# Row sums inverted before the turn, spread by TensorE, and attention outputs transposed as bf16, in a fused attention and expert kernel

## The chip, the cores and the metric

The kernel runs on one core of one Trainium2 chip. The metric is device time in microseconds (us). Most executions of a kernel agree within 0.3%. "PE" is TensorE, "PEld" its weight loads, "DVE" VectorE, "ACT" ScalarE, "POOL" GpSimd, "SP" SyncE. The granted clock is the share of full speed at which TensorE was let run.

The kernels ran on more than one chip. The experiments e1 to e4 and e9 to e12 shared one chip, on which the kernel before takes 262.21 us in the first group and 261.33 us in the second. The experiments e5 to e8 ran on a slower chip, where it takes 270.59 us. So I compare ratios to the kernel before on the same chip, and lengths of stages inside one trace.

## The reference

Four batches of eight heads, 768 positions, head size 64. Each query sees the first 8 keys and the last 96, with a bias linear in the distance. The result, 3072 rows of 512, goes to eight experts. Each takes at most 384 rows, assigned greedily by gate logit.

```python
scores = scale * np.matmul(q, k.transpose(0, 1, 3, 2)) + bias      # bias = -slope[h] * distance
scores = np.where(keep, scores, -1000000000.0)                     # global or local keys only
a = np.exp(scores - np.max(scores, axis=-1, keepdims=True))
a = a / (np.sum(a, axis=-1, keepdims=True) + 1e-09)
x = np.matmul(a, v)                                                # then (tokens, heads * dim)
logits = x @ w_gate                                                # order = np.argsort(-logits.flatten())
out[mask_e] = np.maximum(x[mask_e] @ w1[e], 0.0) @ w2[e]           # for each expert e, at most 384 rows
```

## The kernel before

Attention works on sixteen pairs of heads, two pairs to a round `u`. A round makes scores in three groups; ScalarE takes the exponential; VectorE multiplies it by a mask with the bias in it; TensorE multiplies by `v` into `po` and, from the same masked values, makes the row sums and the gate products in one PSUM tile `pr`. ScalarE copies `po` to `oT` (features on partitions, not yet divided by the row sums). The row sums come back to one row per token by a VectorE transpose, so their reciprocal is small:

```python
def sums_out(n, pr):                      # per pair, VectorE
    LT = sp.tile([128, NBLK, 32], FP32, tag="LT")
    nc.vector.transpose(out=LT.rearrange("p b c -> p (b c)"), in_=pr)
    ri[n] = sp.tile([128, NBLK, 2], FP32, tag="ri", name=f"ri{n}", bufs=6)
    nc.vector.reciprocal(ri[n], LT[:, :, 16:18])            # 12 elements a partition
    nc.vector.tensor_tensor(out=Gb[b][...], in0=LT[:, :, 0:16]..., in1=ri[n]..., op=ALU.mult)
    # ... sums over pairs cut
def tok(n, hf):                           # six fp32 transposes a pair, in two halves
    pk = tokpool[0].tile([128, 3, 128], FP32, tag="pt", name=f"pk{n}_{hf}")
    for bb in range(3):
        nc.tensor.transpose(pk[:, bb, :], oTs[n][:, 3 * hf + bb]..., ident)
    return pk
def tok_out(n, hf, pk):                   # divide by the row sums while leaving PSUM, to bf16
    nc.vector.tensor_tensor(out=xs[u][...], in0=pk..., in1=ri[n]..., op=ALU.mult)
    # ... four writes of x to x_tok after the second pair of a round
```

The loop, rounds 2 to 6, in the order given to the engines:

```python
ps = scores(u, 0); expo(u, 0, ps)
kT(u + 1, 0); kT(u + 1, 1)                # transposes of the next k, VectorE
mask(2 * u, 0); mask(2 * u + 1, 0)
av(A); oT_out(A, 0); oT_out(A, 1)         # A, Bp: the two pairs of round u - 1
pr = sums(A)
# ... kA_out, qT, qT_out cut: copies of k and q by ScalarE
sums_out(A, pr)
ps = scores(u, 1); expo(u, 1, ps)
# ... cut
mask(2 * u, 1); mask(2 * u + 1, 1)
for hf in range(2): pk = tok(A, hf); tok_out(A, hf, pk)
av(Bp); oT_out(Bp, 0); oT_out(Bp, 1)
ps = scores(u, 2); expo(u, 2, ps); mask(2 * u, 2)
pr = sums(Bp); sums_out(Bp, pr)
mask(2 * u + 1, 2)
for hf in range(2): pk = tok(Bp, hf); tok_out(Bp, hf, pk)
```

After the loop a last round mixes attention with a first routing of five experts; then come further routing rounds and the experts. The PSUM pool `ps_t` has two buffers, both under the tag `pt`: `pr` and `pk` take turns in them. The scores have two tiles, `ps0` and `ps1`, of two banks each.

The softmax here doesn't subtract the row's maximum and nothing guards it: scores larger than these inputs give would overflow.

## Time and profile before

| | kernel before |
|---|---|
| time, median of 3 | 261.24 us (261.14 to 262.46) |
| span of the profiled execution, granted clock | 259.5 us, 0.989 |
| loop rounds, from first scores to first scores | 16.2 to 16.6 us, at clock 1.00 |
| first k transpose of round 2 | 38.49 us |
| last round, from its first scores to the first routing round | 116.45 to 145.80, so 29.35 us |
| first routing round | 145.80 to 152.06, so 6.26 us |
| from there to the end | 107.44 us |

The lines for this are in the prediction. They show a loop in which TensorE never stops, with VectorE and ScalarE close behind.

### The profile page before, as it was taken

Reading aid. Unit: us, or ns where it says so; the run is one execution under the profiler, and the core shown is the slowest. Engines: PE = TensorE matmul, PEld = TensorE weight load, DVE = VectorE, ACT = ScalarE, POOL = GpSimd, SP = SyncE. Lnnn points to the kernel's source line nnn. Section 1 sums busy time; section 2 is a strip of 40 time slices with the busy share of each in tenths; the row PEclk is TensorE's granted clock in tenths of the full one; section 3 lists DMA queues with packets and bytes.
Section 4 is the critical chain, followed back from the end, with each engine's and each line's share of the span. In section 5 each row is a group of like instructions: output and inputs, shape, how many; then the busy total and the mean of one; then the engine's idle time right before and its main releaser. Section 6 shows DMA issues by size and latency. Waiting matters only on the chain.

```text
span 259.5 us, 7844 instructions
## 1 busy us (share of the span) xinstructions
PE 241.5 (93%) x3331; PEld 180.0 (69%) x3331; DVE 163.0 (63%) x347; ACT 144.0 (55%) x245; POOL 88.3 (34%) x147
## 2 busy tenths in 40 slices
PE   8699979999999999999998999999999999999960
PEld 2467867888788888887787877765677775555520
DVE  3987998898878988679782687773232323223120
ACT  5998959779597795973432332323444442341600
POOL 5050000030180493005018301127884656742240
PEclk9999999999999999999999999999999999999995
DMA  7993597749689499958998999943599999994221
GB/s 259 328 329 79 160 254 207 197 87 279 185 219 269 81 236 244 198 121 131 208 210 180 168 194 204 201 126 98 96 185 252 262 241 275 231 208 180 83 85 47
DMA packets 52569, 49.29 MB, mean 190 GB/s; under 512 B 29744, under 2 KB 44080, under 8 KB 52528
## 3 DMA queue, kind: packets, MB, share of 16 engines
q0 software_dynamic: 15680, 26.22, 49.2%
q1 hardware_dynamic: 36848, 22.50, 31.7%
q8 instruction: 28, 0.46, 0.7%
q14 instruction: 13, 0.11, 0.1%
HBM read 56.05 MB, written 9.44 MB: 252 GB/s over the span
## 4 chain that ended last, share of the span: by engine, by line
PE 43%; DVE 20%; DMA 13%; issue 9%; ACT 8%; POOL 3%; SPq 1%; POOLq 0%; DVEq 0%
PE ph L1395 7%; PE po L443 6%; PE ps L390 6%; PE po L1404 5%; DVE RT L330 5%; DVE P L423 5%; DMA x_tok<-x 4%; DMA out_dram<-ot,idi 4%; POOL out_dram L955 3%; PE poE L998 3%; PE pr L474 3%; PE pk L519 3%; PE phE L982 2%; DMA RT<-x_tok,idiE 2%; DMA RT<-in_q_dram 2%
## 5 line engine op out<-in xcount | busy, mean ns | idle before, releaser
L408 ACT ACTIVATE P<-ps 128x860 f32<-128x860 f32 (+1 forms) x46 | 39.3, 893 | 23.1 <-PE ps L390 22.3
L1398 ACT ACTIVATE hT<-ph 128x256 bf16<-128x256 f32 (+1 forms) x64 | 27.1, 424 | 38.2 <-PE ph L1395 36.3
L390 PE MATMUL ps<-qT,kA 32*128 32x215 f32 (+2 forms) x864 | 43.2, 333 | 2.5 <-ACT qT L355 2.5
L390 PEld LDWEIGHTS ps<-qT,kA 32*128 32x128 f32 x864 | 36.8, 185 | 7.1 <-ACT qT L355 3.0
L443 PE MATMUL po<-P,v 128*64 128x215 f32 (+6 forms) x576 | 41.3, 293 | 0.1
L443 PEld LDWEIGHTS po<-P,v 128*64 128x64 f32 x576 | 34.1, 136 | 8.4 <-issue 3.2
L423 DVE TENSOR_TENSOR P<-P,Wm 128x860 f32<-128x860 f32 (+1 forms) x32 | 32.9, 1043 | 6.7 <-ACT P L408 4.0
L330 DVE STREAM_TRANSPOSE RT<-RT 128x768 f32<-128x768 f32 x28 | 26.2, 959 | 3.4 <-DMA RT<-in_k_dram 3.4
L474 PE MATMUL pr<-P,onesx 128*32 128x192 f32 (+11 forms) x768 | 27.6, 259 | 0.0
L1411 DVE COPY ot<-po 128x512 f32<-128x512 f32 x18 | 12.5, 692 | 23.9 <-PE po L1404 23.9
L955 POOL DMA_INDIRECT out_dram<-ot,idi x19 | 18.6, 981 | 23.2 <-DVE ot L1411 15.8
L474 PEld LDWEIGHTS pr<-P,onesx 128*32 128x32 f32 x768 | 24.7, 109 | 2.4 <-issue 0.3
L1404 PEld LDWEIGHTS <-hT 128*128 128x128 bf16 x152 | 14.4, 98 | 15.5
L340 ACT COPY kA<-RT 128x720 f32<-128x720 f32 (+2 forms) x18 | 24.4, 1354 | 0.2
L1404 PE MATMUL po<-w,hT 128*128 128x512 bf16 x104 | 23.8, 379 | 0.0
L1395 PE MATMUL ph<-xT,w 128*128 128x384 bf16 (+1 forms) x160 | 23.4, 305 | 0.0
L1376 DVE COPY xT<-pxe 128x512 bf16<-128x512 bf16 x17 | 6.6, 421 | 26.0 <-PE pxe L1375 25.6
L947 POOL DMA_INDIRECT xe<-x_tok,idi x19 | 18.3, 962 | 9.8 <-issue 3.7
L448 ACT COPY oT<-po 128x384 f32<-128x384 f32 x32 | 14.8, 491 | 11.2 <-PE po L443 11.2
L1395 PEld LDWEIGHTS <-w 128*128 128x128 bf16 x160 | 15.7, 98 | 7.7
L416 DVE TENSOR_TENSOR P<-P,Wm 128x860 f32<-128x860 f32 x16 | 16.4, 1058 | 6.6 <-ACT P L408 6.6
L519 PE MATMUL pk<-ident,oT 128*128 128x128 f32 x96 | 16.7, 287 | 2.4 <-DVE LT L490 2.2
(247 smaller groups left out, 330.4 us busy)
## 6 DMA issues: line engine op xcount, KB each, us to landing
w<-in_moe_w_dram POOLq DMA_DIRECT2D x10, 1024.0 KB, 11.9
v<-in_v_dram SPq DMA_DIRECT2D x32, 180.0 KB, 3.4
RT<-in_k_dram SPq DMA_DIRECT2D x7, 768.0 KB, 4.5
RT<-in_q_dram SPq DMA_DIRECT2D x7, 768.0 KB, 6.8
w_early<-in_moe_w_dram POOLq DMA_DIRECT2D x8, 512.0 KB, 7.9
x_tok<-x SPq DMA_DIRECT2D x32, 96.0 KB, 3.2
RT<-in_moe_w_dram POOLq DMA_DIRECT2D x2, 1024.0 KB, 18.4
w_early<-in_k_dram SPq DMA_DIRECT2D x1, 768.0 KB
```

What stands on the lines that cost most here:

```text
L330: nc.vector.transpose(out=t, in_=src[:, :, 32 * g : 32 * g + 32])
L340: nc.scalar.copy(out=kA[:, i0:i1, 8:128].rearrange("p i (c j) -> p i c j", j=NJ), in_=t[:, i0 * NC5 : i1 * NC5, :].rearrange("p (i c) j -> ...
L390: nc.tensor.matmul(heads[a][:, o : o + w], lhsT=kA[r, gd, i, :], rhs=qTt[r, gd, KT * i : KT * i + w], start=(gd == 0), stop=(gd == 1), ski ...
L408: nc.scalar.activation(P[:, :, 0 : GW[g]], ps[w_][:, :, 0 : GW[g]], AF.Exp, scale=0.125)
L423: tt(out=P[:, :, 0 : GW[g]], in0=P[:, :, 0 : GW[g]], in1=Wm[:, h0 : h0 + 2, lo : lo + GW[g]], op=ALU.mult)
L443: nc.tensor.matmul(po[n][bk][64 * t : 64 * t + 64, a - QB * bk : z - QB * bk], lhsT=v7[:, t, i, :], rhs=P[:, t, o + a - q0 : o + z - q0], ...
L474: nc.tensor.matmul(o_, lhsT=l_, rhs=r_, start=first[gq], stop=True, skip_group_check=True)
L519: nc.tensor.transpose(pk[:, bb, :], oTs[n][:, 3 * hf + bb].rearrange("c g r -> c (g r)"), ident)
L955: s = nc.gpsimd.indirect_dma_start(out=out[:, :], out_offset=bass.IndirectOffsetOnAxis(ap=ids, axis=0), in_=ot, in_offset=None)
L1395: nc.tensor.matmul(ph[:, 0 : 128 * ns], lhsT=w1_of(e)[:, kc, 128 * fc : 128 * fc + 128], rhs=xT_e[:, kc, 0:ns, :].rearrange("p t n -> p (t ...
L1398: nc.scalar.activation(hT[:, fc, 0 : 128 * ns], ph[:, 0 : 128 * ns], AF.Relu)
L1404: nc.tensor.matmul(po, lhsT=hT[:, fc, 128 * j : 128 * j + 128], rhs=w2_of(e)[:, fc, :], start=(fc == 0), stop=(fc == NFC - 1))
```

## The change

The intent is to take the twelve fp32 transposes of a round off TensorE. The row sums are inverted where they stand, on 192 columns (`rr`). A matmul with a selection matrix spreads them over the features' partitions, in the score banks, which are free for a moment (`R`). VectorE scales `oT` by this while casting it to bf16 (`xb`). TensorE transposes the bf16 tile six times into one bank (`pk`), and ScalarE copies that out as `x`. Pairs 12 to 15 keep the old way, for which their reciprocals are turned back (`rows_out`).

```diff
 def sums_out(n, pr):
-    nc.vector.transpose(out=LT.rearrange("p b c -> p (b c)"), in_=pr)
-    nc.vector.reciprocal(ri[n], LT[:, :, 16:18])
-    nc.vector.tensor_tensor(out=Gb[b][:, :, 2 * j : 2 * j + 2, :], in0=LT[...], in1=ri[n][...], op=ALU.mult)
+    nc.vector.reciprocal(rr[n], pr[:, 0, :])                                  # 192 elements a partition
+    nc.vector.tensor_tensor(out=gn, in0=pr[:, 1, :], in1=rr[n], op=ALU.mult)
+    nc.vector.transpose(out=Gb[b][:, j].rearrange("p b c -> p (b c)"), in_=gn)
+def rows_out(n):                     # pairs 12 to 15 only
+    nc.vector.transpose(out=LTr.rearrange("p b c -> p (b c)"), in_=rr[n])
+    nc.vector.tensor_copy(out=ri[n], in_=LTr...[:, :, :, 0])
+def spread(n):                       # pairs n and n + 1, into the score banks
+    R = [ps_s.tile([128, 2, 512], FP32, tag=f"ps{w_}", name=f"R{w_}_{n}") for w_ in range(2)]
+    for m in (n, n + 1):
+        for gq in range(4):
+            nc.tensor.matmul(R[gq // 2][:, gq % 2, o : o + 192], lhsT=selx[32 * gq : 32 * gq + 32, :],
+                             rhs=rr[m][32 * gq : 32 * gq + 32, :], start=True, stop=True, skip_group_check=True)
+def scale(n):
+    for w_ in range(2):
+        nc.vector.tensor_tensor(out=xbs[n][...], in0=oTs[n][...], in1=Rs[n][w_]..., op=ALU.mult)
+def turn_x(n): ...                   # six bf16 transposes of xbs[n] into one bank
+def x_out(n, pk):
+    nc.scalar.copy(out=xs[u][:, :, 128 * w_ : 128 * w_ + 128], in_=pk)
 # in round u:
 mask(2 * u, 0); mask(2 * u + 1, 0); av(A)
+spread(A - 2); scale(A - 2); scale(A - 1)
 # oT_out(A), pr = sums(A)
+pk = turn_x(A - 2)                   # x_out(A - 2, pk) among ScalarE's copies
 # sums_out(A, pr), second score group, second masks
-for hf in range(2): pk = tok(A, hf); tok_out(A, hf, pk)
 av(Bp)
+pk = turn_x(A - 1)                   # x_out(A - 1, pk) behind the third group's exponentials
 # third score group, sums_out(Bp), last mask
-for hf in range(2): pk = tok(Bp, hf); tok_out(Bp, hf, pk)
 # last round: spread(10), scale(10), scale(11) ahead of the second score group, then turn_x and x_out
 # cut: ones matrix of 16 columns a head, gate sums over two axes, two constants' memory shared
```

The `x` of a pair is now made one round later than before.

## The prediction

> **What bounds the kernel now.** I read the page first (shares, then the chain), then a table of busy time by stretch, cut where each round of the attention loop starts, then one round in order of time, then single forms. The page gives TensorE most of the span, but the chain changes hands between TensorE and VectorE:
>
> ```profile
> PE 241.5 (93%) x3331; PEld 180.0 (69%) x3331; DVE 163.0 (63%) x347; ACT 144.0 (55%) x245; POOL 88.3 (34%) x147
> ...
> PE 43%; DVE 20%; DMA 13%; issue 9%; ACT 8%; POOL 3%; SPq 1%; POOLq 0%; DVEq 0%
> ```
>
> The table by stretch has, after each stretch and its length, the busy time of PE, PEld, DVE, ACT and POOL. The first two lines are loop rounds (u=4 and 6), the third is the last round with the early routing, up to the first routing round:
>
> ```profile
> 67.60:83.78 16.18, 16.15 (x310) 13.61 (x309) 13.45 (x23) 12.95 (x18) 6.56 (x13) 1.00 0.84 212
> ...
> 100.23:116.45 16.22, 16.19 (x309) 13.69 (x308) 12.90 (x21) 12.95 (x18) 1.66 (x4) 1.00 0.87 169
> 116.45:145.80 29.35, 27.53 (x534) 22.44 (x533) 20.31 (x62) 10.96 (x18) 12.82 (x16) 1.00 0.97 174
> ```
>
> A round takes 16.2 us and TensorE is busy in all of it, at full clock. VectorE does 13 to 14.7 us and ScalarE 13: they follow, with little room. The timeline of round 5 shows how close (VectorE, then TensorE):
>
> ```profile
> 89.16 1.98 DVE L423 TENSOR_TENSOR P<-P,Wm 128x860 f32<-128x860 f32 x2
> 91.95 0.34 DVE L490 STREAM_TRANSPOSE LT<-pr 128x192 f32<-128x192 f32 x1
> 92.32 0.23 DVE L492 RECIPROCAL ri<-LT 128x12 f32<-128x12 f32 x1
> 92.59 0.26 DVE L495 TENSOR_TENSOR Gb<-LT,ri 128x96 f32<-128x96 f32 x1
> ...
> 89.88 1.74 PE L390 MATMUL ps<-qT,kA 32*128 32x215 f32 x32
> 92.34 0.55 PE L519 MATMUL pk<-ident,oT 128*128 128x128 f32 x3 [0.25 <-DVE LT L490]
> 95.28 1.97 PE L390 MATMUL ps<-qT,kA 32*128 32x215 f32 x48
> ```
>
> The second score group (89.88) runs while VectorE still masks the first. It needs nothing from VectorE in this round. That slack is what the change spends.
>
> **What the Trainium skill says.** "VectorE: DVE Perf Modes", section "First, the fixed hardware budget", says that reciprocal is a hardware iterative divide with a repeat count, unlike the one-result-a-cycle operations. It gives no rate; the trace does, in the list of forms:
>
> ```profile
> L492 DVE RECIPROCAL ri<-LT 128x12 f32<-128x12 f32 x16 | 3.7, 228 | 0.6
> L567 DVE RECIPROCAL rnE<-s 128x5 f32<-128x5 f32 x1 | 0.2, 190 | 0.0
> L569 DVE TENSOR_TENSOR me<-s,rnE 128x10 f32<-128x10 f32 x1 | 0.2, 169 | 0.0
> ```
>
> Five elements take 190 ns and twelve 228, so (228-190)/7 = 5.4 ns each, where a plain operation of ten takes 169. The page agrees in kind. "TensorE: Matmul & The Clock Gate", "Weight-path perf modes": fast weight load needs 128 columns and a dtype other than fp32. The trace agrees: loading an fp32 transpose's data takes 140 ns and a bf16 one's 98; three fp32 transposes hold the chain 0.55 us, eight bf16 ones 0.45. The same page, Part 3, "The mechanism": matmuls on different row groups overlap. The 32 score matmuls last about 356 ns each and take 1.67 us together, which agrees; the four spreading matmuls use four row groups too. "PSUM — Partial Sum Buffer", "PSUM bank collisions raise a hardware error": the hardware does not stall on a bank in use, software must order the accesses. So borrowing the score banks puts real waits in the program. No run here shows a collision.
>
> **The change, part by part.** The built program's order confirms the parts; durations are from the profile of before.
>
> TensorE per round loses twelve fp32 transposes (0.81 us from start to the next work for the first six, 1.05 for the other six: 1.9 us). It gains eight spreading matmuls (192 against 215 columns at 1.67/32 us: 0.4 us) and twelve bf16 transposes (0.45/8 each, 0.7 us, plus about 0.2 per switch of dtype). About 0.5 us less.
>
> ScalarE gains two PSUM copies of 768 columns. From 384 columns in 0.49 us and 860 in 0.885: about 0.81 us each, 1.6 a round, to 14.6.
>
> VectorE: scaling is four operations of 384 columns, as before (0.5 us each). The chain after the sums changes from transpose, reciprocal of 12, multiply of 96 (0.38+0.23+0.26 plus two gaps of 0.03: 0.93 us) to reciprocal of 192 (0.16+192x0.0054 = 1.20 us), multiply of 192 (0.36) and transpose (0.34), with gaps 1.95 us. That is 1.0 us per pair, 2.0 a round, 16 over all sixteen pairs. VectorE then has about 16 us of work in a round of 16.2.
>
> The order does worse than the load. The spread row goes into the score banks, so the second score group waits for four scalings, and those stand behind two k transposes (1.75) and two masks (1.9) on VectorE. The last mask pass in turn waits for scores made after that. This closes a ring:
>
> - end of scaling, second score group 1.75, attend 2.45, bf16 transposes 0.5, third score group 1.9: 6.6
> - first exponential to the mask of the third group 0.95 and 1.05, hiding the 2.0 of the row sums: 2.15 with latency
> - new VectorE chain 1.95, mask 1.0, k transposes 1.75, masks 1.9, scaling 1.9: 8.5
>
> Together 17.2 us, before the gate reduction (0.85 in rounds 2, 4 and 6) and the late constants (0.4, 0.6 and 0.95 in rounds 2 to 4), which stand in the ring as well: 18.4, 17.9, 19.0, 17.2 and 17.2 plus 2.3. Start-up is nearly a wash: two pairs lose four x operations (1.85) and gain 1.0 each, so k transposes of round 2 start at 38.9 instead of 38.5. Adding up, the thirteenth pair's last mask ends near 131 us instead of 119.8: 11 us late. In this loop TensorE waits some 2 to 3 us per round.
>
> Last round, by the same laying out: masks (1.9), cut statistics (2.6), four scalings (1.9), before the second score group may start, at 137.4 against 123.5, so 3 us more. Then the chains of pairs 12 and 13 are longer (1.0 each) with 0.55 each for turning the reciprocals back. The five early row ids come at about 150 against 134.8; their gathers still need some 6 us. Pair 15's chain, alone at the end, adds 1.0, and its turned reciprocals 0.55 before the first routing minimum. The first routing round starts near 161 instead of 145.7: about 16 later. From there nothing is changed and I expect the rest to move as a block. 261.2 + 16 = 277; a layout by hand keeps every latency I assume, so I take 275.
>
> **The rivals.** (1) Reciprocal runs at one element a cycle (0.4 us) and the 38 ns are something else. For it: only two sizes are seen, and one input is strided. Against: the plain operations of 5 and 10 elements differ by nothing. The ring is then 16.4 plus extras, rounds average 17.6, the tail loses some 3: 268 to 270. (2) TensorE remains the bound, VectorE and ScalarE catch up in their idle time, and the 0.5 us per round is won, with no fp32 transposes left in the loop: 257 to 260. For it: TensorE is 99% busy in every round. Against: the ring, which has no free step, and 16 us of VectorE work. (3) The ring holds but the loss is partly hidden: x of pair 11 is now written some 17 us later, while 4.5 MB of weights are on their way (the last x write took 11.3 us under such load); had that write been the limit of the gathers before, a later round start with quieter queues gives some back. Before, the write ended at 133.7 and the ids at 134.8, so little: 271 to 274.
>
> **Range and chances.** The ring and the chain both point the same way, and even the cheap reciprocal leaves the ring. Rival 1 (15%) and 3 set the low end at 266.5; an under-counted tail the high end at 281. Rival 2 gets what is left. Faster 0.03, within 2% 0.10, slower 0.87.
>
> **What would show it.** Right: the reciprocal of 192 elements takes 1.1 to 1.3 us; loop rounds of 17 to 19 us with TensorE idle before the second score group, put down to the scaling; VectorE busy 15 to 16.5 us a round; the early gathers start near 150 us. Wrong: a reciprocal near 0.4 us, rounds at or under 16.5 us, TensorE still without gaps, or a tail (first routing round to end) that changes by more than 2 us.

## The result and the profile after

The changed kernel takes 285.25 us (median of 4, 283.83 to 286.1) against 261.19 us for the kernel before beside it. The ratio is 1.0903, with a 95% interval of 1.0839 to 1.0967: slower. A ratio is the mean time of one kernel's fast runs over that of the other's of the same rounds, so it is not quite the ratio of the medians. The direction was right. The time lies outside the range, 4 us above its high end.

The page of the changed kernel has these shares of the span and this chain:

```profile
PE 251.3 (89%) x3415; PEld 188.6 (67%) x3427; DVE 183.8 (65%) x355; ACT 154.0 (55%) x257; POOL 93.0 (33%) x156
...
PE 44%; DVE 29%; DMA 10%; issue 8%; POOL 3%; ACT 2%; SPq 1%; POOLq 0%
```

VectorE's share of the chain went from 20% to 29% of a longer span. That is the ring of the prediction. But TensorE's busy time also grew, by 10 us, though it was to lose work. The table by stretch says why. It cuts the loop rounds from one first k transpose to the next. The first two lines are rounds 3 and 5, the third runs from the last mask of pair 13 to the first routing round, the fourth is the first routing round. The first numbers are the stretch and its length; the number after the five engines' busy times is the granted clock:

```profile
57.61:76.75 19.14, 17.11 (x318) 14.62 (x316) 15.93 (x24) 14.62 (x20) 2.23 (x9) 0.91 0.71 175
...
97.50:116.45 18.95, 16.35 (x300) 13.61 (x296) 15.28 (x22) 13.63 (x18) 11.54 (x24) 0.91 0.68 162
...
136.20:167.04 30.84, 25.54 (x499) 20.76 (x496) 24.44 (x60) 10.55 (x17) 8.61 (x11) 1.00 0.84 154
167.04:175.22 8.18, 7.53 (x68) 6.68 (x68) 5.61 (x20) 2.20 (x5) 0.14 (x2) 0.79 1.16 203
```

In the kernel before the clock was 1.00 in every one of these stages. Now the two loop rounds of the table show 0.91, round 4, left out here, 0.92, and the first routing round 0.79. The timeline shows where (round 5 on VectorE, then round 5 on TensorE, then two lines of round 6 on TensorE):

```profile
97.50 1.82 DVE L340 STREAM_TRANSPOSE RT<-RT 128x768 f32<-128x768 f32 x2
99.26 1.97 DVE L433 TENSOR_TENSOR P<-P,Wm 128x860 f32<-128x860 f32 x2
101.15 1.94 DVE L558 TENSOR_TENSOR xb<-oT,R 128x384 bf16<-128x384 f32 x4
...
103.90 1.31 DVE L501 RECIPROCAL rr<-pr 128x192 f32<-128x192 f32 x1
105.25 0.36 DVE L503 TENSOR_TENSOR gn<-pr,rr 128x192 f32<-128x192 f32 x1
...
96.74 0.93 PE L551 MATMUL R<-rr,selx 32*128 32x192 f32 x16
...
102.22 0.51 PE L565 MATMUL pk<-ident_bf,xb 128*128 128x128 bf16 x6 [2.55 <-DVE xb L558]
102.77 3.60 PE L400 MATMUL ps<-qT,kA 32*128 32x215 f32 x32
...
121.16 0.51 PE L565 MATMUL pk<-ident_bf,xb 128*128 128x128 bf16 x6 [0.74 <-DVE xb L558]
121.72 2.19 PE L400 MATMUL ps<-qT,kA 32*128 32x215 f32 x32
```

In brackets stands how long the engine was idle before a line, and which instruction ended that. VectorE goes through k transposes, masks and scaling without a pause, and TensorE, which needs the scaled tile, stands still for 2.55 us. That was foreseen. The next line was not: the second score group then takes 3.60 us. After a pause of 0.74 us, one round later, the same 32 records take 2.19. The table by stretch gives a clock of 0.59 from 102.77 to 106.30, 0.56 from 62.30 to 66.20 (after a pause of 2.03 us) and 0.63 from 82.02 to 85.29 (after 1.37 us).

The list of forms shows the parts (busy us and mean ns of one, then the idle time before it; four lines picked out):

```profile
L501 DVE RECIPROCAL rr<-pr 128x192 f32<-128x192 f32 x16 | 21.5, 1342 | 4.4 <-PE pr L487 4.2
...
L506 DVE STREAM_TRANSPOSE Gb<-gn 128x192 f32<-128x192 f32 x16 | 6.1, 379 | 0.6
...
L433 DVE TENSOR_TENSOR P<-P,Wm 128x862 f32<-128x862 f32 x16 | 16.8, 1050 | 13.7 <-ACT P L418 13.7
...
L565 PE MATMUL pk<-ident_bf,xb 128*128 128x128 bf16 x72 | 6.4, 227 | 9.8 <-DVE xb L558 9.8
```

The reciprocal of 192 elements takes 1.34 us. VectorE in turn waits 13.7 us for exponentials (L433), five times, once a round (the timeline has 1.91 to 3.53 us each): the ring closes, and neither engine is busy all the time. TensorE gave up 0.81 and 1.05 us of fp32 transposes a round and took on 0.93 us of spreading and twice 0.51 us of bf16 transposes. That is an even exchange.

### The profile page after: what moved, and what is told of

Same layout as the page of the kernel before. It is cut to its first block, busy times and chain, and to the rows that moved or that the text cites. A ratio compares the mean times of both kernels' runs of the same rounds, so it can differ in the third digit from the quotient of the medians.

```text
span 282.6 us, 8071 instructions
## 1 busy us (share of the span) xinstructions
PE 251.3 (89%) x3415; PEld 188.6 (67%) x3427; DVE 183.8 (65%) x355; ACT 154.0 (55%) x257; POOL 93.0 (33%) x156
## 4 chain that ended last, share of the span: by engine, by line
PE 44%; DVE 29%; DMA 10%; issue 8%; POOL 3%; ACT 2%; SPq 1%; POOLq 0%
PE ps L400 10%; DVE P L433 8%; PE ph L1442 6%; DVE RT L340 6%; PE po L453 5%; PE po L1451 5%; DVE rr L501 4%; DMA out_dram<-ot,idi 4%; PE pr L484 3%; POOL out_dram L1002 3%; DMA x_tok<-x 3%; PE poE L1045 3%; PE phE L1029 3%; DMA RT<-in_q_dram 2%; DVE xb L558 2%
## 5 line engine op out<-in xcount | busy, mean ns | idle before, releaser
L400 PE MATMUL ps<-qT,kA 32*128 32x215 f32 (+2 forms) x864 | 50.8, 358 | 5.0 <-ACT qT L365 2.7
L400 PEld LDWEIGHTS ps<-qT,kA 32*128 32x128 f32 x864 | 42.6, 198 | 11.1 <-ACT qT L365 3.2
L433 DVE TENSOR_TENSOR P<-P,Wm 128x860 f32<-128x860 f32 (+1 forms) x32 | 32.8, 1041 | 16.4 <-ACT P L418 13.7
L453 PE MATMUL po<-P,v 128*64 128x215 f32 (+6 forms) x576 | 42.8, 299 | 0.2 <-DVE P L433 0.2
L453 PEld LDWEIGHTS po<-P,v 128*64 128x64 f32 x576 | 34.8, 140 | 10.0 <-issue 3.9
L501 DVE RECIPROCAL rr<-pr 128x192 f32<-128x192 f32 x16 | 21.5, 1342 | 4.4 <-PE pr L487 4.2
L1451 PE MATMUL po<-w,hT 128*128 128x512 bf16 x99 | 22.8, 379 | 0.2
L994 POOL DMA_INDIRECT xe<-x_tok,idi x19 | 18.4, 969 | 9.8 <-DMA out_dram<-ot,idi 3.3
L365 ACT COPY qT<-RT 128x768 f32<-128x768 f32 (+1 forms) x11 | 16.4, 1487 | 2.1 <-DVE RT L340 2.1
```

Of the source, the lines that this page charges most:

```text
L400: nc.tensor.matmul(heads[a][:, o : o + w], lhsT=kA[r, gd, i, :], rhs=qTt[r, gd, KT * i : KT * i + w], start=(gd == 0), stop=(gd == 1), ski ...
L433: tt(out=P[:, :, 0 : GW[g]], in0=P[:, :, 0 : GW[g]], in1=Wm[:, h0 : h0 + 2, lo : lo + GW[g]], op=ALU.mult)
L453: nc.tensor.matmul(po[n][bk][64 * t : 64 * t + 64, a - QB * bk : z - QB * bk], lhsT=v7[:, t, i, :], rhs=P[:, t, o + a - q0 : o + z - q0], ...
L501: nc.vector.reciprocal(rr[n], pr[:, 0, :])
L1451: nc.tensor.matmul(po, lhsT=hT[:, fc, 128 * j : 128 * j + 128], rhs=w2_of(e)[:, fc, :], start=(fc == 0), stop=(fc == NFC - 1))
```

## The experiments

Twelve kernels ran, all with correct results. All were slower than the kernel before, except e7 (unclear), e8, e10 and e11 (the same) and e9 (one run). My theory after the result: the ring and the longer reciprocal chain are as predicted, and what is missing from the sum is the clock, which falls after TensorE's pauses. The rivals: the ring was mis-sized; the tail was; or the chain is not what costs.

**e1_fill: is it the clock?** The waiting TensorE is given bf16 matmuls with no use, into the bank that the transposes then take. Nothing else changes.

```diff
-def turn_x(n):
-    pk = ps_t.tile([128, NBLK, 128], BF16, tag="pt", name=f"pk{n}")
+def turn_x(n, fill=0):
+    pkf = ps_t.tile([128, 512], FP32, tag="pt", name=f"pk{n}")
+    for _ in range(fill):            # 6, 6, 6 and 3 in rounds 3 to 6
+        nc.tensor.matmul(pkf, lhsT=ones_bf, rhs=ones_bf[:, 0:1].to_broadcast([128, 512]), start=True, stop=True)
 pr = sums(15)
+warm(5)                              # five more ahead of the first routing round
```

> The changed kernel with bf16 filler matmuls put into TensorE's pause before the first bf16 transposes of rounds 3 to 6 (6, 6, 6 and 3 of 512 columns, about 0.24 us each) and five before the first routing round. Nothing that VectorE does is altered. Clock theory (the pauses of 1.4 to 2.6 us make the granted clock fall, and the second score group of rounds 3, 4 and 5 then takes 3.25 to 3.6 us instead of 2.2): those groups come back to about 2.2 us at clock 1.00, the first routing round to about 6.5 us from 8.2, and the time falls by 4 to 6 us to 279 to 281. Rival (the groups are slow because VectorE holds the score banks): they stay at 3.2 to 3.6 us and the time stays at 284 to 287.

It took 279.31 us (278.63 to 280.99), ratio 1.0672 (1.0599 to 1.0744), as the clock theory had it. Adding work made the kernel faster. Its stretches, rounds 3, 4 and 5 and the first routing round:

```profile
57.73:75.67 17.94, 17.22 (x323) 13.80 (x322) 15.82 (x24) 14.56 (x20) 2.21 (x9) 1.00 0.76 184
75.67:94.79 19.12, 19.02 (x355) 15.42 (x352) 16.86 (x27) 15.29 (x22) 6.55 (x13) 1.00 0.75 182
94.79:112.10 17.31, 16.07 (x306) 12.89 (x302) 15.25 (x21) 13.49 (x18) 11.52 (x24) 1.00 0.78 187
...
163.20:169.63 6.43, 6.05 (x72) 5.14 (x69) 5.43 (x19) 2.79 (x6) 0.00 (x0) 1.00 1.14 204
```

With the clock at 1.00 the rounds 2 to 5 take 18.60, 17.94, 19.12 and 17.31 us. The prediction had 18.4, 17.9, 19.0 and 17.2. The changed kernel itself took 18.60, 19.14, 20.75 and 18.95. So the ring was right to 0.2 us a round, and each fall of the clock cost 1.20, 1.63 and 1.64 us on top. e1 is not at full clock everywhere: its last round has no filler, and there the clock fell (0.50 from 138.08 to 141.50) where that of the changed kernel did not.

**e12_after_again: does the ratio hold, and does the clock fall in the same places?** The changed kernel once more, with a comment added, so its lines are numbered one higher.

```diff
+# the changed kernel once more, on this chip
 (all else the same)
```

> The changed kernel once more, to have it on the same chip as the others. If the ratio to the kernel before holds from chip to chip it is 1.08 to 1.10 (1.090 where it was first timed); if the chip matters to how far the granted clock falls, it lies outside of that, up to 1.11.

286.48 us, ratio 1.094 (1.0888 to 1.0992), on the chip of e1. So the useless matmuls of e1 are worth 2.7% there. The timeline of round 4, first in the profile of after, then in this one:

```profile
81.47 0.51 PE L565 MATMUL pk<-ident_bf,xb 128*128 128x128 bf16 x6 [1.37 <-DVE xb L558]
82.02 3.34 PE L400 MATMUL ps<-qT,kA 32*128 32x215 f32 x32
```

```profile
82.81 0.51 PE L566 MATMUL pk<-ident_bf,xb 128*128 128x128 bf16 x6 [1.37 <-DVE xb L559]
83.36 2.19 PE L401 MATMUL ps<-qT,kA 32*128 32x215 f32 x32
```

The same pause of 1.37 us brought the clock down in one execution and not in the other. The pauses of 2.03 and 2.5 us in rounds 3 and 5 did so in both (3.61 and 3.15 us here). The pause of 2.33 us in the last round did so here (2.86 us) and not in the first profile (2.19), and one of 2.34 us in round 2 did not here (2.19). So it is no fixed threshold of pause length.

Cut finer, the traces tell what it is. In the seven traces of the changed kernel, e1 to e5 and e12, from 20 to 178 us, every fall of the clock reads 0.50 and lasts 3.42 to 3.44 us or about twice that (6.84 to 6.86). The falls of one trace begin whole multiples of 3.41 us apart: in the changed kernel at 35.10, 62.42, 82.90, 103.38 and 168.22 us, the later ones 8, 14, 20 and 39 times 3.413 us after the first. So the clock is set for windows of 3.41 us at a time, and what goes with a fall is the idle time of TensorE inside the window before it. The table by stretch of the changed kernel, cut at these windows (the number after the length is TensorE's busy time):

```profile
99.95:103.37 3.42, 1.11 (x14) 0.83 (x18) 3.42 (x7) 2.69 (x7) 3.32 (x5) 1.00 0.84 245
103.37:106.79 3.42, 3.42 (x33) 2.78 (x34) 3.35 (x5) 2.82 (x4) 3.03 (x10) 0.50 1.24 232
137.50:140.91 3.41, 1.89 (x56) 1.44 (x48) 3.10 (x13) 0.00 (x0) 0.00 (x0) 1.00 1.19 193
140.91:144.33 3.42, 2.55 (x38) 2.08 (x38) 3.35 (x7) 0.95 (x2) 0.00 (x0) 1.00 1.21 211
```

The pause of round 5 left 2.31 us idle in one window, and the next window ran at half clock. The pause of 2.34 us in the last round was cut by a window's edge into 1.52 and 0.87 us, and nothing fell. Over the seven traces all 11 full-clock windows with 1.8 us or more of idle time were followed by a fall, and none with less than 1.1 us was; between 1.14 and 1.75 us it went both ways (1.42 us in round 4 of the changed kernel: a fall; 1.40 us in e12: none).

**e2_scale_first: the order on VectorE.** The scaling is put ahead of the two masks.

```diff
-mask(2 * u, 0)
-mask(2 * u + 1, 0)
 av(A)
 spread(A - 2)
 scale(A - 2)
 scale(A - 1)
+mask(2 * u, 0)
+mask(2 * u + 1, 0)
```

> The changed kernel with the four scalings put ahead of the two first mask passes of each round on VectorE; the same instructions otherwise. Ring theory (the scalings stand behind two masks of 1.9 us, and the score banks wait for them): the ring loses 1.9 us, TensorE's pause before the transposes falls under 0.7 us and with it the clock loss; rounds come to 16.5 to 17.3 us, set by VectorE's load, and the time to 270 to 275. Load theory (VectorE has too much to do, in whatever order): rounds stay at 18.5 to 20 us and the time at 282 to 286.

277.67 us, ratio 1.0586 (1.0498 to 1.0673). The direction is as expected, the size was missed. TensorE's wait for the scaled tile fell from 9.8 to 2.9 us, and the second score groups of the loop take 1.74 to 2.19 us. But the third score group is now held up inside itself, 2.72 us instead of 1.96, and the line names ScalarE:

```profile
49.28 2.72 PE L400 MATMUL ps<-qT,kA 32*128 32x215 f32 x48 [0.27 <-ACT P L418]
```

ScalarE has the copy of `x` (0.79 us) in front of those exponentials. The last round was not reordered; its pause of 2.33 us and a second score group of 3.08 us are still there.

**e3_small_recip: the chain without the long reciprocal.** The row sums are turned first, 12 are inverted in place, and the turned block is turned back to be spread. The rest of the change stays.

```diff
-nc.vector.reciprocal(rr[n], pr[:, 0, :])
-nc.vector.tensor_tensor(out=gn, in0=pr[:, 1, :], in1=rr[n], op=ALU.mult)
-nc.vector.transpose(out=Gb[b][:, j]..., in_=gn)
+nc.vector.transpose(out=LT..., in_=pr)
+nc.vector.reciprocal(ri[n], L4[:, :, :, 8])              # 12 elements, in place in LT
+nc.vector.tensor_tensor(out=Gb[b][...], in0=L4[...], in1=ri[n]..., op=ALU.mult)
+nc.vector.transpose(out=rr[n], in_=LT...)                # behind the gates, pairs under 12
```

> The changed kernel with the reciprocal taken on 12 elements after the transpose, as before the change, in place, and the transposed block turned back for the spreading matmuls (one transpose of 0.38 us more, off the chain to the gates). The chain behind the sums is then 0.93 us instead of 2.1. Chain theory (the reciprocal of 192 elements at 1.34 us is half of the loss): the ring loses about 0.8 us and VectorE 1.4 us a round, pauses come near or under 1.4 us, pairs 12 to 15 lose their extra chain and turning (about 1.6 us each, part of it hidden): 270 to 277. If only the order around the score banks matters: 281 or more.

274.91 us, ratio 1.049 (1.0427 to 1.0554), within what was expected. Against 1.094 for the whole change on this chip, the long reciprocal carries some 4.5% of the time, its share of the clock's falls included: the pauses in rounds 2 to 5 are 0.44 to 1.55 us, and only one score group of the loop takes over 2.2 us (3.11).

**e4_both: e2 and e3 together** (the two edits above).

> Both edits together: scalings ahead of the masks, and the reciprocal on 12 elements. If the ring and the chain are the whole loss in the loop, TensorE is again the bound with rounds of 16.2 to 16.6 us at full clock; what is left is the last round (scalings of pairs 10 and 11 before its second score group, about 3 us, and the later write of x): 262 to 267. If something else costs (the spreading matmuls, the copies on ScalarE), 268 or more.

272.97 us, ratio 1.0408 (1.0326 to 1.0489): a miss. From round 3 on the loop is at full clock, but its rounds are 17.04, 17.02, 17.52 and 17.04 us, from one first score group to the next, not 16.2. The wait that took over is ScalarE's again, in the list of waits of the weight loads (us in total, times, longest):

```profile
PEld ps L400 <- ACT P L418: 6.2, 13, 0.8
```

The rest is in the last round: from its first scores (121.41) to the first routing round (158.29) it takes 36.9 us, against 29.35 before. There two pairs' scaling stands in front of the second score group, TensorE pauses 2.82 us, and the group takes 3.03 us. The clock is 0.50 from there for two windows, 133.52 to 140.38: up to 3.4 us of the last round's loss is the clock (half of 6.86, TensorE being busy all that time).

**e6_tail_old and e7_both_tail_old: the last round.** Pairs 10 and 11 go the old way, within round 6; e6 is after with this, e7 is e4 with this.

```diff
 # round 6, ahead of av(Bp) and behind the last mask:
+for hf in range(2): pk_ = tok(A, hf); tok_out(A, hf, pk_)      # A is 10; the same for Bp, 11
 # last round:
-spread(10); scale(10); scale(11)
-x_out(10, turn_x(10)); x_out(11, turn_x(11))
```

> The changed kernel with pairs 10 and 11 done the old way inside round 6 (reciprocals turned back, fp32 transposes, scaling in token order), so that the last round has no spreading and no scaling before its second score group and x of pair 11 is written some 10 us earlier. Tail theory (the last round lost 5 us on these two pairs): the gathers of the early rows wait for the row ids again and not for the write of x, the stretch from the last score group 0 to the first routing round shrinks by 4 to 5 us, and round 6 grows by about 1 us: 280 to 282.5. If the tail's loss is only in the chains of pairs 12 to 15: 284 to 286.

> Scalings ahead of the masks, reciprocal on 12 elements, and pairs 10 and 11 the old way. The run with the first two edits still had rounds of 17.0 us and a last round 7.5 us longer than before, with a 2.8 us TensorE pause and a fallen clock in it. If these two pairs are the cause: the last round comes back to about 29.5 to 31 us and the time to 266 to 268. If the last round stays long: 270 to 273.

e6: 291.92 us, ratio 1.0738 (1.065 to 1.0825). e7: 277.22 us, ratio 1.0243 (1.0194 to 1.0291), unclear, as the interval spans 2%. As ratios both are near what was expected. Against 1.0903 and 1.094 for the change, and 1.0408 for e4, the tail of the change costs 1.6 to 2.0% (across two chips, so roughly). In e7 the last round takes 29.6 us (123.85 to 153.48) where e4 took 36.9, and round 6 takes 20.6 where e4 took 17.0. So the last round's loss, 7 us, was real (up to 3.4 of it the clock, which does not fall there in e7), and 3.5 us come back in the round before.

**e5_chain_only: the chain alone.** The kernel before, with the new chain and `rows_out` for all pairs, and the old fp32 transposes.

```diff
 # sums, sums_out as in the change; for every pair:
 sums_out(n, pr)
+rows_out(n)
 # tok and tok_out as before
```

> The kernel before with only the new chain behind the sums (reciprocal of 192 elements, multiply, transpose) and, so that the old fp32 transposes and scalings can stay, the reciprocals turned back for all pairs (0.55 us each). No spreading, nothing borrowed from the score banks. VectorE's load per round rises by 2 x (1.2 + 0.55) = 3.5 us to about 17.3. Load theory: rounds of about 17 to 17.5 us, 266 to 272 in all. Ring theory as the main cause: TensorE shows no pause of more than 1 us in the loop and its clock stays 1.00, so that this half costs clearly less than the whole change: 266 to 272 too, but with full clock; if the chain alone made pauses with a falling clock, 275 or more.

292.53 us on the slower chip, ratio 1.0787 (1.0731 to 1.0844): a miss for the two main theories, and in size what the last case foresaw, a chain that makes pauses by itself. The list of TensorE's waits (us in total, times, longest) says where it went:

```profile
PE pk L522 <- DVE gn L493: 17.8, 12, 2.5
```

`pr` and `pk` share two PSUM buffers. Before, `pr` came free after one transpose of 0.34 us; here after the reciprocal and the multiply, 1.7 us. The second half of the fp32 transposes waits for that. The list of waits of the whole change has no such line: `turn_x` takes one bank instead of two halves. So this run measures a cost that the change does not have, and does not weigh the chain within it. It shows that the same three instructions cost whatever waits for them. It also shows that a pause need not bring the clock down: of nine pauses of 1.43 to 2.45 us between 36 and 135 us, one (1.96 us) was followed by a fall (0.50 from 106.12 to 109.54).

**e9_recip: the reciprocal by itself.** Reciprocals and plain multiplies are added where the expert stage begins; their results are not used.

```diff
+for w in (12, 24, 48, 96, 192):
+    nc.vector.reciprocal(ro[:, 0:w], ui[:, 0:w])
+for w in (48, 192):
+    nc.vector.tensor_tensor(out=ro[:, 0:w], in0=ui[:, 0:w], in1=ui[:, 0:w], op=ALU.mult)
```

> The kernel before, with reciprocals of 12, 24, 48, 96 and 192 elements a row and two plain multiplies of 48 and 192 added on VectorE where the expert stage begins; results unchanged. Theory (the reciprocal's time is proportional to its elements, at the rate seen in the traces: 1.34 us for 192 in the changed kernel): about 0.16 us plus 6 ns an element, so 0.23, 0.30, 0.45, 0.74 and 1.3 us. Rival (192 took long because it read the PSUM bank or ran against TensorE's writes, and the reciprocal itself runs like any other one-operand instruction at about 1 ns an element): 0.1, 0.1, 0.13, 0.18 and 0.28 us, like the multiplies of the same size. The time of the whole is 1 to 4 us above the kernel before at most.

262.63 us, one run, state unknown; only the durations count here. From the list of forms:

```profile
L1383 DVE RECIPROCAL ro<-Ub 128x192 f32<-128x192 f32 x1 | 1.4, 1354 | 0.0
...
L1383 DVE RECIPROCAL ro<-Ub 128x96 f32<-128x96 f32 x1 | 0.7, 739 | 0.0
...
L1385 DVE TENSOR_TENSOR ro<-Ub 128x192 f32<-128x192 f32 x1 | 0.3, 346 | 0.0
...
L1383 DVE RECIPROCAL ro<-Ub 128x12 f32<-128x12 f32 x1 | 0.2, 220 | 0.0
...
L1385 DVE TENSOR_TENSOR ro<-Ub 128x48 f32<-128x48 f32 x1 | 0.2, 198 | 0.0
```

From 12 to 192 elements the reciprocal gains (1354-220)/180 = 6.3 ns an element, with its operands in SBUF and no one in its way. A multiply gains (346-198)/144 = 1.03 ns. The rival, a reciprocal as quick as any other operation, is out.

**e8_cast: half the idea without the spreading.** VectorE casts the raw `oT` to bf16, TensorE makes six bf16 transposes into one bank, and one operation of 768 columns scales in token order, as before, with the small reciprocals. Pairs 2 to 11 only; the rest is the kernel before, but for two constants' memory, shared as in the change.

```diff
+def cast(n): nc.vector.tensor_copy(out=obs[n], in_=oTs[n])                       # to bf16
+def tok_bf(n): ...                                   # six bf16 transposes of obs[n]
+def tok_bf_out(n, pk): nc.vector.tensor_tensor(out=xs[u][...], in0=pk..., in1=ri[n]..., op=ALU.mult)
+cast(A)                                              # ahead of sums_out(A, pr)
-for hf in range(2): pk = tok(A, hf); tok_out(A, hf, pk)
 av(Bp)
+tok_bf_out(A, tok_bf(A))                             # Bp: cast behind the third exponentials, tok_bf at the end
```

> A version from the kernel before: the gain that the change was after, without spreading. The unscaled outputs of pairs 2 to 11 are cast to bf16 by VectorE (one copy of 768 columns, estimated 0.5 us from a 768 column copy of 0.85 and one of 128 to bf16 of 0.18), transposed as bf16 after the next attend, and scaled in token order as before, in one operation instead of two. TensorE's transposes fall from 1.9 us a round to about 1.0; VectorE gains 0.9 us of work that it has idle. If bf16 transposes are worth anything: rounds of 15.3 to 15.8 us instead of 16.2 and 256 to 259 in all. If VectorE's or ScalarE's order takes the place of the bound: 260 to 263.

269.69 us on the slower chip, ratio 0.9943 (0.9877 to 1.0009): the same. It needs no ring, since nothing of it stands between the masks and the second score group, and its rounds are 15.9 us on average (35.74 to 115.16, five rounds). But the third score group is again stretched, by ScalarE:

```profile
94.44 2.72 PE L390 MATMUL ps<-qT,kA 32*128 32x215 f32 x48 [0.59 <-ACT P L408]
```

**e10_reorder_only and e11_cast_reorder: ScalarE's order.** One copy of ScalarE, the first half of the next `qT` (1.5 us), moves behind the second group's exponentials; in e10 in the kernel before, in e11 in e8.

```diff
 qT(u + 1, 0)
-qT_out(u + 1, 0)
 # sums_out(A, pr), second score group, expo(u, 1, ps)
+qT_out(u + 1, 0)
 qT(u + 1, 1)
```

> The kernel before, with one of ScalarE's copies a round (the query copy, 1.5 us) moved behind the exponentials of the second score group. If that copy, ahead of the exponentials, is what delays the third score group only once the transposes are bf16 (theory: the before kernel is not bound by ScalarE at this point), nothing is gained: ratio 0.99 to 1.01 to the kernel before. Rival: ScalarE's order already costs in the kernel before, and the ratio is 0.97 to 0.985.

> e8_cast (bf16 transposes by a cast of the raw outputs, no spread, scaling in token order as before) with the same copy of ScalarE behind the exponentials. Theory: in e8_cast the third score group waited some 0.3 to 0.6 us for those exponentials, so the rounds go from 15.9 to 15.3 to 15.6 us and the ratio to the kernel before is 0.975 to 0.990. Rival: another wait ends just behind (VectorE's masks, or the copy now late for the next round's first score group), and the ratio stays at 0.990 to 1.0.

e10: 261.35 us, ratio 0.9996 (0.9957 to 1.0035). In the kernel before that copy is in nobody's way. e11: 258.31 us, ratio 0.9875 (0.9838 to 0.9912). The third score group is back at 1.96 us in most rounds:

```profile
61.75 1.96 PE L390 MATMUL ps<-qT,kA 32*128 32x215 f32 x48
```

and the rounds are 15.6 us on average (35.77 to 113.60, five rounds). This is the fastest of all the kernels here. Its gain of 1.25% is clear of the noise, but within the 2% that are called the same. It has the part of the intent that was sound, the bf16 transposes, and none of the spreading.

## Why the prediction was right or wrong

By where the time stands in the traces (us; the predicted column is from the text, its third row being the 16 us in all less the two rows above, 0.4 and 8.9):

| stretch | before | predicted | after | e1, full clock in rounds 2 to 5 |
|---|---|---|---|---|
| start to k transposes of round 2 | 38.49 | 38.9 | 39.01 | 39.13 |
| rounds 2 to 5 | 63.58 | 72.5 | 77.44 | 72.98 |
| round 6 to the second routing round | 49.99 | 56.7 | 58.77 | 57.52 |
| from there to the end | 107.44 | the same | 107.38 | 107.47 |

**What failed.** It is the step "Together 17.2 us, before the gate reduction", and with it "In this loop TensorE waits some 2 to 3 us per round". The ring was summed with a second score group of 1.75 us and an attend of 2.45, the durations of a TensorE that never pauses, in a loop which by its own account now pauses. The pauses came (0.74 to 2.55 us before the transposes); that they slow the work after them was left out. In the changed kernel the group took 3.25, 3.34 and 3.60 us in rounds 3 to 5, and two of the attends behind it 3.00 and 2.74 instead of 2.52. In the loop this is 77.44-72.98 = 4.5 us. The first routing round, after a pause of 1.59 us, took 8.18 us; e1 took 6.43, so 1.75 us more. Together 6.2 of the 23.1 us between the two spans. The other 16.9 are close to the 16 that were laid out. e1 is the evidence: it adds only work that keeps TensorE busy, and the rounds come to the predicted lengths. In all e1 is 5.5 us shorter (277.1 against 282.6), less than 6.2, as its last round, with its own fall, and its start and end are 0.7 us longer together.

The Trainium skill, "TensorE: Matmul & The Clock Gate", section "HAM oscillation — how this bites in real kernels", tells of this: a matmul kernel with waits between its bursts starts each burst at half clock. Its rule is a gap of more than about 3.4 us, by which pauses of 2 to 3 us look harmless; the prediction does not mention the clock. The section "What's actually happening" has a window of 3.4 us, free-running, and two clocks only, full and half. The traces agree with that part: cut at the windows, the clock reads 1.00 or 0.50. A window at half clock costs 3.42/2 = 1.7 us (an estimate from the length of the falls), and rounds 4 and 5 lost 1.63 and 1.64 us each, though round 3 lost 1.20. They agree with free-running too: the falls last 3.42 us and begin whole windows apart, whatever the loop does. They do not agree with 3.4 us as the shortest harmful gap: 1.8 us of idle time in one window was always enough.

**What was right.** The mechanism: the ring, in the order predicted, with TensorE idle before the bf16 transposes, put down to the scaling. The start-up, 39.01 us against 38.9, although the clock fell there too (35.10 to 38.54), which was not foreseen. The last round: laid out as 30 us from the last mask of pair 13 (131) to the first routing round (161); measured 136.2 to 167.04, so 30.8. The early gathers, laid out for 150, came at 157.54 (see rival 3). The rest moved as a block, to 0.1 us, from the second routing round on; the first was not part of the block.

**What was off and small.** The reciprocal took 1.34 us, not 1.20: the rate of 5.4 ns was taken from two sizes 7 elements apart, and e9 has 6.3. Spreading took 0.93 us a round, not 0.4: the 32 records of a score group are 16 matmuls, so eight spreading matmuls leave 16 records (16 x 1.67/32 = 0.84). Hence TensorE gained nothing where 0.5 us a round was predicted; as TensorE was not the bound any more, this hardly shows. The last term was a deduction: the layout gave 277, and I took 275 because a layout by hand keeps every latency. It had in fact left one out.

**The rivals.** (1) is out by e9. (2), TensorE as the bound, is out by the trace. (3), a write of `x` that hides part of the loss: the first half came true, since the ids were ready at 155.5 us and the early gathers started at 157.54, when the write of `x` had landed. It gave nothing back, as the last row of the table shows.

**What stays open.** Why windows with 1.14 to 1.75 us of idle time went both ways; no run here moved a pause step by step through a window. Why round 3 lost only 1.20 us. How far the clock's falls in e6 account for its time was not separated. The chain's cost inside the whole change, without the clock, was not measured alone: e3 takes away both.

## What to carry to other kernels

A change that makes a saturated TensorE wait, even for 1.4 to 2.5 us at a time, costs the wait, and may then cost 1.2 to 1.75 us more for a slower clock after it (in e3, e4 and e12 one fall lasted twice as long). Here 1.8 us idle within one window of 3.41 us always brought it on, and less than 1.1 us never. Add that to the sum, and test it by filling the pauses with useless matmuls. When work moves between engines, follow which instruction stands in front of which: 1 us more of reciprocal a pair, on an engine that had slack, cost some 4.5% because the next scores waited behind it. Keep the reciprocal on the few elements that need it, and look for the part of an idea (here the bf16 transposes) that adds no wait.

## What the Trainium skill lacked or had wrong

- "TensorE: Matmul & The Clock Gate", "HAM oscillation — how this bites in real kernels": its rule allows gaps up to about 3.4 us. Here pauses of 1.37, 2.03 and 2.55 us were followed by clocks of 0.63, 0.56 and 0.59, and filling them, and the one before the first routing round, took 5.6 us off the way to the second routing round (175.22 to 169.63). What the runs show is idle time inside one 3.41 us window: 1.8 us or more always brought half clock in the next (11 of 11), less than 1.1 us never.
- "VectorE: DVE Perf Modes", "First, the fixed hardware budget": it says how the reciprocal is computed but gives no rate. The runs show 220 ns for 12 elements a partition and 1354 ns for 192, so 6.3 ns an element against 1.03 ns for a multiply, in fp32.
- No page says that an fp32 matmul shows as two records in such a profile. Eight of 192 columns on 32 rows left 16 records here and took 0.93 us, about 0.12 us each.
